# Hash attention into channel mix: wide exps, in-place bits for the first head, joined DMAs and a new order

## The chip, the cores and the metric

One Trainium2 chip, one of its cores. The metric is device time in microseconds of one execution; the same inputs are used each time. The program computes everything in a single launch.

## The reference, cut to what matters

```python
# attention: batch 4, 8 heads, 768 positions, head width 64
q_bits = (einsum('bhsd,dk->bhsk', q, proj) > 0)      # 6 sign bits per row; k_bits alike
mask   = q_bucket[:, :, :, None] == k_bucket[:, :, None, :]
scores = where(mask, scale * q @ k.T, -1e9)
attn   = softmax(scores)                             # over the keys
x      = (attn @ v)  with the heads side by side     # (4, 768, 512)
# channel mix
xk, xr = mixes of x and x shifted by one position, with mu_k and mu_r
k   = max(xk @ w_k, 0)                               # 512 -> 1024
out = sigmoid(xr @ w_r) * ((k * k) @ w_v)
```

A query attends only to the keys whose six sign bits are all equal to its own.

## The kernel before, in words

The 32 heads are handled as 16 pairs, numbered n = 0 to 15, four pairs to a batch. For each pair:

- **Loads.** q and k go to `nat` tiles (three slots), v to `vn`, one DMA each on SP's queue. The first pair is loaded head by head, with k on ACT's queue.
- **Preparation.** The matmul of the scores contracts over 128 partitions: 64 hold q or k times 4 in fp16, six hold the sign bits as large signed numbers, so that one exp with a bias sends every pair of rows with a differing bit to zero. From pair 2 on `add_prep` makes the fp16 value (`hi`, L398) and its rounding error (`lo`, L401) on VectorE, and a transposing DMA on SP turns both (L405). `add_bits` multiplies the turned tile with the projection on TensorE (L427), VectorE takes the signs (L431) and POOL copies them into their six rows, four copies a pair (L443). For pairs in `MERGED` (4 to 15) hi, lo and the DMA treat q and k together, for 2 and 3 one side at a time.
- **The first two pairs** (`FIRSTS`) go through `add_prep_turn` instead: TensorE turns the fp32 tile (L478), ACT copies it negated to SBUF (L483), TensorE multiplies it with the projection (L489), VectorE makes hi (L467) and writes the signs (L497) beside it, TensorE turns the fp16 tile (L512) and VectorE or ACT copies it to its place (L517, L519). Pair 0 goes head by head, pair 1 with both heads at once.
- **Scores and exp.** `add_scores` cuts the 2 x 6 x 768 = 9,216 columns of a pair into nine pieces of 1,024. Each takes two of the eight PSUM banks (`sc` slots 0 to 3), gets three matmuls (L544) and one exp on ACT (L548).
- **PV.** `add_pv` multiplies the exps with v, 12 matmuls to a step and three steps to a head (L571); VectorE divides (L582 to L589). The result is turned by TensorE (pairs 0 to 3 and 15, L599) or a DMA (L605).
- **Mix.** `add_mix` forms xk and xr on VectorE. After four pairs `add_moe` does a batch's channel mix: L659 with relu on ACT (L663) and the square on VectorE (L666), L679 with tanh (L682), L692, and the product (L699) and store (L702). The very last row block is cut into 256, 128 and 128 columns.

At the start TensorE runs matmuls on zeros: `warm0` to `warm13` (L246, one each) and eight `warmb` (L251, two each), which the order places between other work.

Every `add(...)` registers one operation with its engine, an estimate of its duration and what it reads and writes. The list `ORDER` holds the numbers of these operations in the order in which they are issued, and `BANKS` the PSUM place of each operation that takes one. Each engine thus runs its own operations strictly in the order of that list, and waits in that order. So do SP's DMAs. An operation that waits for data or for its PSUM banks holds all that follow on its engine.

In the order before, 22 warm-up matmuls stand ahead of the first L478. On ACT all of `ey0...`, `evt0k0` and `ey1k0` and `evt0k1` stand before the first exp (`sc0_1`); on PE the first L659 stands behind five of the nine score pieces of pair 5 and behind the bits block of pair 6.

## Time and profile before

| | us |
|---|---|
| median of 3 runs (241.7 to 242.24) | 242.17 |
| the profiled execution | 242.0 |
| its span, first to last instruction | 240.2 |
| PE busy | 234.1 |
| ACT busy | 181.9 |
| DVE busy | 179.8 |
| POOL busy | 99.7 |

PE is TensorE's matmuls, PEld its weight loads, DVE VectorE, ACT ScalarE, POOL GpSimd, SP the engine that issues most DMAs. The page cuts the span in 40 slices of 6 us and gives each engine's busy share in tenths. A row of a timeline has start, length, engine, line, operation and, after x, how many like instructions were merged; in brackets stand the idle time before it and who ended it. A row of a group has, behind its count, the busy time, the mean nanoseconds of one, and the engine's idle time before the group with who ended it. A group's mean contains the pipeline's latency, so the pace of a series is read from starts, or from busy time over count.

### The profile page before, as it was taken

The page shows a single profiled execution, that of the slowest core. Times are in us where ns is not written, and L with a number is a line of the kernel's source. Part 1 is how long each engine was busy: PE and PEld are TensorE (multiplying, and loading weights), DVE is VectorE, ACT ScalarE, POOL GpSimd, SP SyncE. Part 2 cuts the span into 40 slices and gives each one's busy share as a digit, 9 for nine tenths or more (in the row PEclk, how much of TensorE's full clock was granted, in tenths as well). Part 3 has the DMA queues.
Part 4 walks back from the last instruction along what each step waited for, and adds up shares of the span by engine and source line. Part 5 has one row for each costly group of instructions (what it writes and reads, how often), then busy time and mean ns, then how long its engine had stood idle before and what let it go on. Part 6 is the DMA issues. An engine that isn't in the chain of part 4 may idle for free.

```text
span 240.2 us, 6251 instructions
## 1 busy us (share of the span) xinstructions
PE 234.1 (97%) x2515; PEld 147.8 (62%) x2532; DVE 179.8 (75%) x388; ACT 181.9 (76%) x242; POOL 99.7 (41%) x148
## 2 busy tenths in 40 slices
PE   8999999999999999999999999999999999999994
PEld 6985776776766565656456656665566564455442
DVE  3488789999998898989868896887167867348232
ACT  2699999999999999889779999677884640256320
POOL 4064979989934899438087302550000000000000
PEclk9999999999999999999999999999999999999999
DMA  6989999999999999988999989401500401210333
GB/s 225 304 222 274 232 242 260 279 197 362 279 253 284 273 213 294 249 302 206 276 163 241 249 177 234 136 0 26 173 0 3 120 3 44 87 46 1 131 135 131
DMA packets 72605, 44.00 MB, mean 183 GB/s; under 512 B 54912, under 2 KB 67584, under 8 KB 72576
## 3 DMA queue, kind: packets, MB, share of 16 engines
q1 hardware_dynamic: 72208, 43.20, 70.9%
q8 instruction: 20, 0.33, 0.6%
q10 hardware_dynamic: 368, 0.39, 0.5%
q14 instruction: 9, 0.07, 0.1%
HBM read 24.12 MB, written 6.29 MB: 127 GB/s over the span
## 4 chain that ended last, share of the span: by engine, by line
PE 92%; ACT 5%; issue 1%; DVE 0%
PE ps_all L544 25%; PE ps_all L692 17%; PE ps_all L659 16%; PE ps_all L571 14%; PE ps_all L679 8%; ACT pt L548 4%; PE ps_all L427 4%; PE ps_all L489 2%; PE ps_all L512 1%; PE ps_all L478 1%; ACT kr L663 1%; PE ps_all L251 1%; PE ps_all L246 1%; PE ps_all L599 1%; PE ps_all L566 1%
## 5 line engine op out<-in xcount | busy, mean ns | idle before, releaser
L548 ACT ACTIVATE pt<-ps_all 128x1024 bf16<-128x1024 f32 x144 | 138.4, 1041 | 10.9 <-PE ps_all L544 10.3
L544 PE MATMUL ps_all<-a 128*128 128x256 f16 (+1 forms) x384 | 79.2, 325 | 0.5 <-ACT pt L548 0.3
L443 POOL COPY a<-bx 6x384 f32<-6x384 f32 x56 | 38.9, 695 | 34.4 <-DVE bx L431 19.6
L544 PEld LDWEIGHTS <-a 128*128 128x128 f16 x384 | 34.0, 98 | 23.5 <-issue 4.6
L659 PE MATMUL ps_all<-xk,wk 128*128 128x384 bf16 x256 | 48.3, 326 | 0.1
L571 PEld LDWEIGHTS <-pt 128*128 128x128 bf16 x1152 | 42.5, 97 | 8.0 <-issue 0.5
L692 PE MATMUL ps_all<-wv,k 128*128 128x512 bf16 (+2 forms) x199 | 45.6, 362 | 0.5
L571 PE MATMUL ps_all<-va,pt 128*128 128x65 bf16 x1152 | 44.8, 193 | 0.0
L663 ACT ACTIVATE kr<-ps_all 128x384 bf16<-128x384 f32 x64 | 29.4, 491 | 16.0 <-PE ps_all L659 14.4
L659 PEld LDWEIGHTS <-wk 128*128 128x128 bf16 x256 | 24.2, 98 | 17.0 <-issue 0.6
L692 PEld LDWEIGHTS <-k 128*128 128x128 bf16 x208 | 19.3, 98 | 18.9 <-issue 0.3
L699 DVE SCALAR_TENSOR_TENSOR os<-rs,ps_all 128x512 f32<-128x512 f32 (+2 forms) x26 | 16.5, 643 | 19.0 <-PE ps_all L692 13.7
L682 ACT ACTIVATE rs<-ps_all 128x512 f32<-128x512 f32 x24 | 14.3, 602 | 20.5 <-PE ps_all L679 14.1
L666 DVE TENSOR_TENSOR k<-kr 128x384 bf16<-128x384 bf16 x64 | 23.2, 389 | 8.3 <-ACT kr L663 8.3
L401 DVE SCALAR_TENSOR_TENSOR nh<-nat,nh 128x1536 f16<-128x1536 f32 (+1 forms) x16 | 27.0, 1694 | 0.2
L679 PE MATMUL ps_all<-wr,xr 128*128 128x512 bf16 x88 | 23.2, 379 | 0.4
L356 POOL TENSOR_TENSOR vt<-vn 128x384 f32<-128x384 f32 x12 | 17.8, 1485 | 12.5 <-DMA vn<-in_v_dram 11.7
L589 DVE TENSOR_TENSOR ob<-ps_all,rc 128x384 bf16<-128x384 f32 x32 | 17.5, 553 | 1.4 <-DMA xt<-ob 0.8
L431 DVE TENSOR_SCALAR bx<-ps_all 128x768 uint16<-128x768 uint16 x14 | 13.4, 956 | 5.3 <-PE ps_all L427 4.7
L398 DVE TENSOR_SCALAR nh<-nat 128x1536 f16<-128x1536 f32 (+1 forms) x16 | 15.8, 985 | 0.3 <-PE ps_all L512 0.2
L679 PEld LDWEIGHTS <-xr 128*128 128x128 bf16 x96 | 9.0, 98 | 9.0
L380 DVE SCALAR_TENSOR_TENSOR va<-ps_all,vn 128x384 bf16<-128x384 f32 x24 | 12.7, 548 | 0.5 <-PE ps_all L375 0.2
(77 smaller groups left out, 188.9 us busy)
## 6 DMA issues: line engine op xcount, KB each, us to landing
vn<-in_v_dram SPq DMA_DIRECT2D x16, 384.0 KB, 5.1
out_dram<-os SPq DMA_DIRECT2D x23, 256.0 KB, 2.3
nat<-in_k_dram SPq DMA_DIRECT2D x15, 384.0 KB, 4.7
nat<-in_q_dram SPq DMA_DIRECT2D x15, 384.0 KB, 5.2
wst<-in_moe_w_k_dram SPq DMA_DIRECT2D x2, 512.0 KB, 7.0
wst<-in_moe_w_r_dram SPq DMA_DIRECT2D x2, 512.0 KB, 5.8
wst<-in_moe_w_v_dram SPq DMA_DIRECT2D x2, 512.0 KB, 4.4
k<-in_moe_w_k_dram SPq DMA_DIRECT2D x1, 512.0 KB, 4.4
```

Source lines behind the costliest of these rows:

```text
L356: e.tensor_tensor(out=vt[:, :, :, 0:E], in0=src[:, :, 0:3, 0:E], in1=src[:, :, 3:6, 0:E], op=ALU.add)
L401: nc.vector.scalar_tensor_tensor(out=nh[:, :, D:P], in0=nat.rearrange("p j (c d) -> p (j c) d", d=D), scalar=QS, in1=nh[:, :, 0:D], op0=AL ...
L443: nc.gpsimd.tensor_copy(side_a[side][n % NAQ][D : D + NB, j, :].bitcast(FP32), bx_t[sx][32 * i : 32 * i + NB, :].bitcast(FP32))
L544: nc.tensor.matmul(ps[:, lo - s * STEP : hi - s * STEP], side_a["k"][sa][:, j, jc * P : (jc + 1) * P], side_a["q"][sa][:, j, q0 : q0 + hi ...
L548: nc.scalar.activation(out=pt_t[sp][:, s * STEP : (s + 1) * STEP], in_=ps_t[plan.slot[nm]], func=AF.Exp, bias=EBIAS, scale=ESC)
L571: nc.tensor.matmul(oo[:, ic * 65 : ic * 65 + 65], pt_t[sp][:, o : o + P], va_t[sa][:, j, jc, 0 : D + 1], start=(not uc and ic == 0 and jc ...
L589: nc.vector.tensor_tensor(out=ob_t[so][:, :, j * D : (j + 1) * D], in0=oo[:, :, 0:D], in1=rc_t[sr][:, 1, :].unsqueeze(2).to_broadcast([P, ...
L659: nc.tensor.matmul(ps[:, 0:HALF], wk_sb[:, d, fc * P : (fc + 1) * P], xk_t[mx[d]][:, h * HALF : (h + 1) * HALF], start=(d == 0), stop=(d = ...
L663: nc.scalar.activation(out=kr_t[sk], in_=sm(nm)[:, 0:HALF], func=AF.Relu, scale=0.5 ** 0.5)
L666: nc.vector.tensor_tensor(out=k2_t[s2][:, h * HALF : (h + 1) * HALF], in0=kr_t[sk], in1=kr_t[sk], op=ALU.mult)
L679: nc.tensor.matmul(sm(nr), xr_t[mx[d]][:, c * P : (c + 1) * P], wr_sb[:, d, :], start=(d == 0), stop=(d == NDC - 1))
L692: nc.tensor.matmul(sm(nv)[:, x0:x1], k2_t[(b * NFC + fc) % NK2][:, c * P : (c + 1) * P], wv_sb[:, fc, x0:x1], start=(fc == 0), stop=(fc == ...
```

## The change

- **Wide exps.** For pairs 1 to 3 (`WIDE`) the 9,216 columns go in six pieces of 1,536 over three PSUM banks; where each starts is given by bank. Dependences on the exps are kept by bank (512 columns) instead of by piece of 1,024.
- **First head in place.** For head 0 of pair 0 (`DIRECT`) the new `add_direct` turns each half (384 columns) of one head to 64 partitions, ACT copies it negated, VectorE writes the fp16 value from PSUM straight into the score operand, a matmul with the projection placed in columns 64 to 69 (`pwx`) puts the bits on partitions 64 to 69, and VectorE writes their signs straight into the operand's rows. There is no fp16 turn for it.
- **Second pair split.** Pair 1 (`TURNED`) is now prepared by `add_prep`: hi and lo per side, then TensorE turns the fp16 tiles and VectorE copies them; its bits come from `add_bits` and POOL's four row copies. It no longer has its own fp32 turn and copy on ACT.
- **Joined DMAs.** `MERGED` begins at pair 2.
- **Warm-up.** `warm` matmuls go from 14 to 8; the separate exp that touched ACT's table and its memset are gone. One of two large memsets of `nh` is gone, two small ones come with `add_direct`.
- **New order** and new bank list. On PE 14 warm-up matmuls stand ahead of the first turn. On DVE the order at the start is: hi of head 1 (k, q), q's two halves with pair 1's q hi after them, k's first half, pair 1's q lo, signs of q half 0, k half 0, q half 1, then k half 1, extraction, sign, pair 1's k hi, extraction, k lo, five copies, hi and lo of pair 2, and then the signs of pair 1. On SP the load of pair 1's q is third, after the two heads of pair 0's q. On PE the first L659 stands behind five score pieces of pair 5, the last of which takes the banks of the eleventh exp after pair 3, and the bits block of pair 6 follows it. The last row block of the output is still cut, but a whole block of 512 columns (`v3_4`) is now the last to be computed and stored.

The wide pieces of pairs 1 to 3, in the order of their exps, with the banks that they take:

```
pair 1: 5-7, 0-2, 5-7, 0-2, 3-5, 5-7
pair 2: 1-3, 5-7, 1-3, 0-2, 4-6, 0-2
pair 3: 4-6, 0-2, 4-6, 0-2, 0-2, 3-5
```

```diff
-    NWARM = 14
+    NWARM = 8
...
-    MERGED = tuple(range(4, 16))
-    FIRSTS = (0, 1)
+    MERGED = tuple(range(2, 16))
+    FIRSTS = (0,)
+    TURNED = (1,)
...
+    DIRECT = ((0, 0),)
+    WIDE = (1, 2, 3)
...
+    pwx = buf([P, 96], FP32, "pwx")
...
+            if n in TURNED:
+                for j in range(2):
...
+                    add("PE", 0.48, tp, r=["idh", ("nhh", side, sh, j), ("nhl", side, sh, j)], w=[(nm,)], take=("sm", nm, 0), name=nm)
+                    add("DVE", DVE_C(S, 2), ev, r=[(nm,)], w=[("a", side, sa, j)] + [("ab", side, sa, j, h) for h in range(2)], give=[nm], name="ev" + nm)
+                continue
...
+    def add_direct(n, side, j):
...
+            def tp(ny=ny, h=h):
+                for c in range(3):
+                    nc.tensor.transpose(sm(ny)[0:D, c * P : (c + 1) * P], nat[:, j, (3 * h + c) * D : (3 * h + c + 1) * D], idf)
+
+            def e32(ny=ny, cols=cols):
+                nc.scalar.activation(out=a32[:, cols], in_=sm(ny)[0:D, 0:HALF], func=AF.Copy, scale=-1.0)
+
+            def hi(ny=ny, cols=cols):
+                nc.vector.tensor_scalar(out=a[0:D, j, cols], in0=sm(ny)[0:D, 0:HALF], scalar1=QS, scalar2=None, op0=ALU.mult)
+
+            def bb(nx=nx, cols=cols):
+                nc.tensor.matmul(sm(nx)[0:96, 0:HALF], pwx[0:D], a32[:, cols], start=True, stop=True)
+
+            def sg(nx=nx, cols=cols):
+                nc.vector.tensor_scalar(out=a[D : D + NB, j, cols].bitcast(U16),
+                                        in0=sm(nx)[D : D + NB, 0:HALF].bitcast(U16).rearrange("p (c e) -> p c e", e=2)[:, :, 1],
+                                        scalar1=0x8000, scalar2=bq, op0=ALU.bitwise_and, op1=ALU.bitwise_or)
...
+    def parts(n):
+        step = 3 * BANK if n in WIDE else STEP
+        return [(lo, lo + step) for lo in range(0, 2 * NSC * S, step)]
...
+            def place(nm=nm, a0=a0, a1=a1):
+                b0 = plan.slot[nm] * (STEP if a1 - a0 == STEP else BANK)
+                return ps_all[:, b0 : b0 + a1 - a0]
...
+        add("POOL", 0.2, lambda: nc.gpsimd.tensor_copy(pwx[0:D, D : D + NB], pw[0:D, 0:NB]), r=["pw0"], w=["pwx"], port=1, name="pjcp")
```

68 lines of the change are left out of this document (45 added, 23 removed), and 119 rows, old and new, of tables (BANKS, ORDER).

## The prediction

> **What bounds the kernel now.** I read the page first: the busy rows, then the 40 slices.
>
> ```profile
> PE 234.1 (97%) x2515; PEld 147.8 (62%) x2532; DVE 179.8 (75%) x388; ACT 181.9 (76%) x242; POOL 99.7 (41%) x148
> ...
> PE   8999999999999999999999999999999999999994
> ...
> DVE  3488789999998898989868896887167867348232
> ACT  2699999999999999889779999677884640256320
> ```
>
> TensorE is never idle for long, and ScalarE and VectorE are full as well in the first third. A busy PE is not proof of a bound, since the ends of matmuls are modelled, so the windows of the first half come next (columns: stretch, its length, then busy time and instructions of PE, PEld, DVE, ACT, POOL, then granted clock, DMA share, GB/s).
>
> ```profile
> 12.00:16.00 4.00, 4.00 (x36) 3.25 (x35) 3.65 (x7) 4.00 (x5) 1.78 (x2) 1.00 0.70 229
> 36.00:42.00 6.00, 6.00 (x97) 3.99 (x95) 5.90 (x11) 6.00 (x8) 5.64 (x6) 1.00 1.09 261
> 48.00:60.00 12.00, 11.99 (x181) 8.13 (x174) 11.56 (x27) 11.79 (x14) 10.93 (x13) 1.00 1.17 279
> 204.00:216.00 12.00, 11.95 (x66) 6.37 (x65) 4.49 (x11) 4.90 (x10) 0.00 (x0) 1.00 0.18 67
> ```
>
> From 36 to 60 us PE, ACT, DVE and POOL are all between 91% and 100%. After 200 us PE alone is full. So the end is PE's work plus whatever PE loses early, and early on PE lives on what ACT gives it: until the first matmul of the channel mix there is nothing to do but scores, PV and bits. The timeline of ACT and PE shows the early rhythm.
>
> ```profile
> 11.60 4.69 ACT L548 ACTIVATE pt<-ps_all 128x1024 bf16<-128x1024 f32 x5
> 16.13 0.85 ACT L483 ACTIVATE pt<-ps_all 128x768 f32<-128x768 f32 x1
> 16.82 2.00 ACT L548 ACTIVATE pt<-ps_all 128x1024 bf16<-128x1024 f32 x2
> 19.06 35.03 ACT L548 ACTIVATE pt<-ps_all 128x1024 bf16<-128x1024 f32 x38 [0.24 <-PE ps_all L544]
> ...
> 57.64 0.65 PE L659 MATMUL ps_all<-xk,wk 128*128 128x384 bf16 x3
> ```
>
> The first exp starts at 11.60. From 19.06 on 38 exps run in 35.03 us without a gap, 0.922 us each. Seven were done before, so the 36 of the first four pairs end at 19.06 + 29 x 0.922 = 45.8 us. The channel mix (L659) starts at 57.64. These three times are the marks that I carry through.
>
> **The change, part by part.**
>
> **Start of PE's real work.**
>
> ```profile
> DMA to landing us min/median/max: 3.0/3.4/3.8
> ...
> 0.73 0.88 SPq L321 DMA_DIRECT2D nat<-in_q_dram  x2
> ...
> 1.19 0.61 PE L251 MATMUL ps_all<-k 128*128 128x256 bf16 x2 [1.19 <-DVE k L243]
> 1.59 0.85 PE L246 MATMUL ps_all<-k 128*128 128x256 bf16 x3
> ...
> 4.99 0.38 PE L246 MATMUL ps_all<-k 128*128 128x256 bf16 x2
> 5.21 1.47 PE L478 MATMUL ps_all<-pt,nat 128*128 128x128 f32 x12
> 6.51 1.41 PE L489 MATMUL ps_all<-pw,pt 128*128 128x12 f32 x12
> ...
> 57.21 0.59 PE L544 MATMUL ps_all<-a 128*128 128x512 f16 x3
> ...
> 5.73 1.64 ACT L483 ACTIVATE pt<-ps_all 128x384 f32<-128x384 f32 x4 [2.19 <-PE ps_all L478]
> ...
> 5.44 0.58 POOL L710 TENSOR_SCALAR npj<-pw 64x6 f32<-64x6 f32 x2 [2.16 <-DMA pw<-in_proj_dram]
> ```
>
> Today 22 warm-up matmuls fill 1.19 to 5.21, 0.2 us apart at first (1.59 less 1.19 for two). The new order puts 8 + 3 x 2 = 14 ahead of the first transpose, so it can start near 1.19 + 14 x 0.215 = 4.2 us; q's first half lands before that (the first loads of q land 3.0 to 3.8 us after issue, which begins at 0.73). PE starts **1.0 us earlier**. The second pair's own fp32 transposes and bit matmuls go and one bits block comes, the first head gets twelve smaller transposes and four matmuls of 384 fp32 columns. No row shows that matmul. A 128-column fp32 transpose takes 0.11 (twelve between 5.21 and 6.51), a 12-column fp32 matmul as much; so the ends are 0.11 and 0.65 (six such transposes), and I take 0.33, three of them for three times the columns. It lies beside VectorE's chain either way, as follows.
>
> **The first head on VectorE.** The three transposes of a half (0.33), their latency (0.2) and ACT's copy (0.41, a quarter of 1.64) make the first half ready for DVE at 4.2 + 0.94 = 5.1 to 5.2. DVE's new order is: two halves of q, hi of pair 1's q, one half of k, lo of pair 1's q, three sign operations, and only then may the first scores go. The durations:
>
> ```profile
> L380 DVE SCALAR_TENSOR_TENSOR va<-ps_all,vn 128x384 bf16<-128x384 f32 x24 | 12.7, 548 | 0.5 <-PE ps_all L375 0.2 <-issue 0.2
> L398 DVE TENSOR_SCALAR nh<-nat 128x1536 f16<-128x1536 f32 x12 | 12.9, 1078 | 0.1
> L401 DVE SCALAR_TENSOR_TENSOR nh<-nat,nh 128x1536 f16<-128x1536 f32 x12 | 23.3, 1941 | 0.1
> L401 DVE SCALAR_TENSOR_TENSOR nh<-nat,nh 128x768 f16<-128x768 f32 x4 | 3.7, 954 | 0.1
> L398 DVE TENSOR_SCALAR nh<-nat 128x768 f16<-128x768 f32 x4 | 2.8, 704 | 0.2 <-PE ps_all L512 0.2
> L517 DVE COPY a<-ps_all 128x768 f16<-128x768 f16 x6 | 3.3, 546 | 0.7 <-PE ps_all L512 0.4
> L497 DVE TENSOR_SCALAR nh<-ps_all 128x36 uint16<-128x36 uint16 x4 | 0.8, 191 | 3.2 <-PE ps_all L489 3.2
> L431 DVE TENSOR_SCALAR bx<-ps_all 128x768 uint16<-128x768 uint16 x14 | 13.4, 956 | 5.3 <-PE ps_all L427 4.7 <-ACT kr L663 0.7
> L443 POOL COPY a<-bx 6x384 f32<-6x384 f32 x56 | 38.9, 695 | 34.4 <-DVE bx L431 19.6 <-issue 9.9 <-POOL vt L356 1.5
> ...
> 10.90 0.79 ACT L519 COPY a<-ps_all 128x768 f16<-128x768 f16 x1
> ```
>
> A 384-column pass out of PSUM on fewer partitions is not among them: between 0.27 (half of L517's 768) and 0.55 (L380); I take 0.5, near L380's. Then 6 x 0.5 + 0.6 (hi) + 0.92 (lo) = 4.5, and the scores may go at 9.8 (0.1 for the late load of pair 1). PE needs until about 9 for what stands before them, so DVE decides. Scores of 1,024 columns take 0.43 (57.21 to 57.64) and 0.16 more until the last is out (0.59): first exp at **10.4 instead of 11.6**.
>
> **Second pair.** Its bits now come late. Before them on DVE stand one half of k, two sign operations, two small extractions (2 x 0.2, L497), hi, lo, five evictions, and then hi and lo of pair 2 in joined form: 2 x 0.5 + 0.4 + 0.6 + 0.92 + 5 x 0.55 + 1.08 + 1.94 = 8.7. So L431 for pair 1 runs from 18.5 to 19.45; its matmuls are ready two microseconds sooner, the queue is what holds it. Two row copies on POOL (0.70 each, L443) are needed before any score of pair 1: 20.85. Scores of 1,536 columns 0.64 (one and a half times 0.43) plus 0.2: first wide exp at 21.7. ACT is done with pair 0 at 10.4 + 9 x 0.922 + 0.8 (one eviction, L519) = 19.5. **ACT waits 2.2 us** there, where before it waited 0.24.
>
> **Wide exps.** From 0.41 at 384 columns to 0.922 at 1,024 is 0.80 ns a column, so 1,536 columns cost 1.33 (upper end 1.38, one and a half times 0.922). 18 x 1.33 = 23.9 against 27 x 0.922 = 24.9: **1.0 us gained**. But two wide buffers take six of the eight banks. Where a score tile's banks overlap those of the exp just before it, PE cannot fill ahead and ACT waits for a whole refill. By the new bank list that is so three times: the sixth tile of pair 1 (banks 5 to 7 after 3 to 5), the fourth of pair 2 (0 to 2 after 1 to 3), the fifth of pair 3 (0 to 2 twice). Each costs 0.64 + 0.16 and the signals, some 0.85: **2.6 us lost**. So the first four pairs end at 21.7 + 23.9 + 2.6 = 48.2 instead of 45.8.
>
> The Trainium skill, ScalarE: Activation LUTs, Rules for kernel authors, budgets about 0.3 us for every ACTIVATE beside 0.83 ns an element. By that nine instructions fewer would save 2.7 us, an estimate from that page, and the end would come 1.7 us sooner than below. This trace disagrees: 0.922 for 1,024 columns leaves 0.07 to 0.10 beside the elements when exps follow one another.
>
> **To the channel mix.**
>
> ```profile
> 31.46 0.77 PE ps_all L427 x16
> ```
>
> Its first matmul stands behind a score tile that needs the eleventh exp after pair 3 done: 48.2 + 11 x 0.922 + 0.45 = 58.8, 1.2 later than 57.64. The seventh pair's bits block, 0.77, now comes after it rather than before. PE has the same work left otherwise: **+1.9 us**. DVE agrees: 8 x 0.5 for the first head, two lo of 0.92 and a bits pass of 0.96 for pair 1 come, seven passes of 0.2 to 0.55 go; that adds over 3 us to an engine that is 96 to 98% busy there.
>
> **The end.**
>
> ```profile
> 234.97 1.71 PE L692 MATMUL ps_all<-wv,k 128*128 128x128 bf16 x20
> ...
> 236.71 0.42 DVE L699 SCALAR_TENSOR_TENSOR os<-rs,ps_all 128x256 f32<-128x256 f32 x1 [0.43 <-PE ps_all L692]
> ...
> 233.50 1.49 DVE L699 SCALAR_TENSOR_TENSOR os<-rs,ps_all 128x512 f32<-128x512 f32 x2 [1.90 <-PE ps_all L692]
> ...
> out_dram<-os SPq DMA_DIRECT2D x23, 256.0 KB, 2.3
> ...
> out_dram<-os SPq DMA_DIRECT2D x1, 128.0 KB, 1.7
> ```
>
> Today the last piece is 256 columns wide: 0.42 on DVE and a 128 KB store of 1.7. In the new order the last is a whole row block of 512: 0.69 (other rows of L699; two make 1.49) and 2.3. That is 0.27 + 0.6 = **+0.9 us**. The pieces of 128 and 256 columns go ahead of it and are hidden.
>
> Edits at nothing: the joined transposes of pairs 2 and 3 (their results wait for banks and DVE), the removed table operation (ACT idles at that point; if uncovered 0.2), the new POOL copy of the projection (0.29, half of L710's 0.58, hidden behind PE's transposes; a late one delays the signs one for one), and the order of loads.
>
> **Sum.** The profiled execution took 242.0 us, its span 240.2, the rest is outside; the median of the runs is 0.17 above it. 242.0 + 1.9 + 0.9 = 244.8; against the median 245.0. I say **244.9**.
>
> **Rivals.**
>
> *Forecast: ACT's chain sets the channel mix late,* 243.2 to 247. The lower end has DVE's passes at 0.27 (2 us sooner at pair 1, less 0.4 that ACT then limits); the upper has 1.38 for a wide exp (0.9) and waits for banks of 1.2 (1.0). Chance 0.50.
>
> *The lag is swallowed (faster).* One mechanism at one place, the first L659: if PE rather than ACT paces the way there, the earlier start counts. For it speaks the 97% of PE, and that the same share holds in every slice. Against it speaks the gapless ACT row. Then PE arrives 1.0 sooner, and about 1 us of prep is gone: 57.64 - 2.0 = 55.6, and the end is 242.0 - 2.0 + 0.77 + 0.27 = 241.0 if the larger store hides its 0.6. The price is ACT's whole 3 us; with the store hidden it decides from L659 before 56.1. Chance 0.22, from 239.8 to 241.6. Halfway, within 0.2% (0.5 us, about what a measurement of this kernel can tell from no change): 0.10.
>
> *The head is not shortened* (it does not do what it says). DVE's queue stands behind the load of pair 1's q, issued third.
>
> ```profile
> DMA to landing us min/median/max: 3.8/4.9/8.9
> ```
>
> Issued at 1.7 it lands between 5.5 and 10.6 by these extremes; at 7.5 hi and lo of pair 1 hold q's signs 1.2 longer, and all marks move: 246.1. Chance 0.12.
>
> *A cold start.* The warm-up rows show 0.21 us a matmul early and 0.11 at 4.99; with eight fewer, and pauses behind ACT and DVE, the fast pitch could come late. Twelve transposes and four fp32 matmuls at double time cost up to 2 us: 247. Chance 0.06. The Trainium skill, TensorE: Matmul & The Clock Gate, What's actually happening, says that the clock opens after about 3.4 us of sustained work; by that rule 14 matmuls (3.0 us) just miss it, so it speaks for this rival. By that rule, the trace agrees: the pitch has halved by 4.99, and no run here shows a shorter warm-up.
>
> **How the numbers follow.** Slower 0.50 + 0.12 + 0.06 = 0.68, same 0.10, faster 0.22. The range leaves out about a tenth on either side: 240.6 to 247.3. The forecast's own range is 243.2 to 247.
>
> **What would show it.** The first exp near 10.4; L431 for pair 1 near 18.5 behind a joined lo; an ACT wait near 2 us before the first wide exp; three ACT waits on L544 near 0.85 among the wide exps; wide exps 1.33 apart; the first L659 near 58.8; a last store of 256 KB. Wrong it is if ACT runs through from pair 0 to pair 1, if the wide tiles never wait, or if L659 comes before 57.6 all the same.

## The result and the profile after

The changed kernel takes 249.93 us (median of 3 runs, 248.65 to 249.94) against 242.17 before: **slower**, ratio 1.0309 [1.0256, 1.0362]. The direction is the one forecast, the size is not: 7.8 us instead of 2.7, and 249.93 lies outside the range. The profiled execution took 249.93, its span is 248.1. Medians below hold all executions of a kernel; ratios leave out those over 1.5% above its fastest, among them the profiled one of `e2_bits_first`, one of 407.93 us in `e16_before_joined`, and two of four in `e14_four_mends`, which has no ratio.

In the changed kernel L609 is the exp (L548 before), L605 the scores (L544), L446 the sign pass (L431), L458 POOL's row copies (L443), L442 the bits' matmul (L427), L719 the channel mix's first matmul (L659), L759 the last product (L699). The page of the changed kernel, with the clock's row:

```profile
PE 234.9 (95%) x2475; PEld 145.2 (59%) x2496; DVE 186.0 (75%) x389; ACT 180.3 (73%) x231; POOL 103.2 (42%) x153
...
PE   7894998999999999999999999999999999999993
...
DVE  4798289999999979998985988896436859545242
ACT  3285788989999999988998898776865642436311
...
PEclk9999799999999999999999999999999999999999
```

PE's busy time is nearly the same (234.9 after, 234.1 before), and the span is 7.9 longer: most of this is idle time of PE, and it stands in the first slices. Two of the windows shown for before:

```profile
36.00:42.00 6.00, 5.56 (x84) 3.60 (x81) 5.91 (x11) 5.14 (x4) 5.50 (x9) 1.00 0.83 189
204.00:216.00 12.00, 11.95 (x84) 6.25 (x83) 8.82 (x20) 4.34 (x8) 0.00 (x0) 1.00 0.06 22
```

From 36 to 42 PE had 6.00 busy and ACT 6.00; now 5.56 and 5.14. After 200 nothing differs for PE. ACT's timeline shows where the gaps are:

```profile
12.18 1.94 ACT L609 ACTIVATE pt<-ps_all 128x1024 bf16<-128x1024 f32 x2 [1.80 <-PE ps_all L605]
...
17.41 4.69 ACT L609 ACTIVATE pt<-ps_all 128x1024 bf16<-128x1024 f32 x5 [0.56 <-PE ps_all L605]
25.38 1.45 ACT L609 ACTIVATE pt<-ps_all 128x1536 bf16<-128x1536 f32 x1 [3.28 <-PE ps_all L605]
27.27 1.45 ACT L609 ACTIVATE pt<-ps_all 128x1536 bf16<-128x1536 f32 x1 [0.44 <-PE ps_all L605]
29.27 4.14 ACT L609 ACTIVATE pt<-ps_all 128x1536 bf16<-128x1536 f32 x3 [0.55 <-PE ps_all L605]
34.30 5.57 ACT L609 ACTIVATE pt<-ps_all 128x1536 bf16<-128x1536 f32 x4 [0.90 <-PE ps_all L605]
40.73 9.51 ACT L609 ACTIVATE pt<-ps_all 128x1536 bf16<-128x1536 f32 x7 [0.86 <-PE ps_all L605]
51.14 15.08 ACT L609 ACTIVATE pt<-ps_all 128x1536 bf16<-128x1536 f32 x15 [0.90 <-PE ps_all L605]
```

Where before one row ran from 19.06 to 54 without a gap, ACT now waits six times from pair 1 on. Seven wide exps in 9.51 are 1.36 each. The last row merges wide and narrow exps: two wide ones end pair 3 at 53.93. The channel mix and the end:

```profile
64.89 0.65 PE L719 MATMUL ps_all<-xk,wk 128*128 128x384 bf16 x3
65.47 0.83 PE L442 MATMUL ps_all<-a,p 128*32 128x512 f16 x16
```

```profile
240.88 0.69 DVE L759 SCALAR_TENSOR_TENSOR os<-rs,ps_all 128x512 f32<-128x512 f32 x1 [0.83 <-DMA out_dram<-os]
...
244.42 0.69 DVE L759 SCALAR_TENSOR_TENSOR os<-rs,ps_all 128x512 f32<-128x512 f32 x1 [0.44 <-issue]
```

The last product ends at 245.11, the span 3.0 later; before it ended at 237.13 and the span 3.1 later. So the larger store adds nothing behind it. The marks, against the prediction:

| us from the span's start | before | predicted | after |
|---|---|---|---|
| first exp | 11.60 | 10.4 | 12.18 |
| first exp of pair 1 | 20.89 | 21.7 | 25.38 |
| pair 3's last exp ends | 45.75 | 48.2 | 53.93 |
| first matmul of the channel mix | 57.64 | 58.8 | 64.89 |
| last matmul ends | 236.68 | 238.6 | 244.33 |

From the channel mix to the last matmul it is 179.0 before and 179.4 after. In this kernel nearly the whole loss (7.25 us) is there when the channel mix begins.

### The profile page after: what moved, and what is told of

Read it like the earlier page. It is cut to its first block, busy times and chain, and to the rows that moved or that the text cites. A ratio compares the mean times of both kernels' runs of the same rounds, so it can differ in the third digit from the quotient of the medians.

```text
span 248.1 us, 6172 instructions
## 1 busy us (share of the span) xinstructions
PE 234.9 (95%) x2475; PEld 145.2 (59%) x2496; DVE 186.0 (75%) x389; ACT 180.3 (73%) x231; POOL 103.2 (42%) x153
## 4 chain that ended last, share of the span: by engine, by line
PE 81%; ACT 7%; DMA 4%; DVE 3%; issue 2%; POOL 1%; ACTq 0%; DVEq 0%; POOLq 0%
PE ps_all L605 21%; PE ps_all L719 17%; PE ps_all L752 16%; PE ps_all L631 11%; PE ps_all L739 8%; ACT pt L609 6%; PE ps_all L442 3%; DMA pw<-in_proj_dram 2%; DMA nat<-in_q_dram 2%; POOL a L458 1%; PE ps_all L484 1%; DVE nh L402 1%; DVE bx L446 1%; PE ps_all L659 1%; PE ps_all L542 1%
## 5 line engine op out<-in xcount | busy, mean ns | idle before, releaser
L609 ACT ACTIVATE pt<-ps_all 128x1024 bf16<-128x1024 f32 (+1 forms) x135 | 138.0, 1102 | 21.3 <-PE ps_all L605 20.8
L605 PE MATMUL ps_all<-a 128*128 128x512 f16 (+1 forms) x384 | 80.1, 328 | 5.0 <-POOL a L458 3.2
L458 POOL COPY a<-bx 6x384 f32<-6x384 f32 x60 | 43.2, 720 | 51.4 <-DVE bx L446 27.7
L605 PEld LDWEIGHTS <-a 128*128 128x128 f16 x384 | 34.2, 98 | 27.2 <-issue 5.5
L631 PEld LDWEIGHTS <-pt 128*128 128x128 bf16 x1152 | 44.0, 98 | 9.1 <-issue 1.1
L719 PE MATMUL ps_all<-xk,wk 128*128 128x384 bf16 x256 | 48.5, 326 | 0.0
L631 PE MATMUL ps_all<-va,pt 128*128 128x65 bf16 x1152 | 46.1, 194 | 0.0
L752 PE MATMUL ps_all<-wv,k 128*128 128x512 bf16 (+2 forms) x195 | 45.0, 361 | 0.7
L723 ACT ACTIVATE kr<-ps_all 128x384 bf16<-128x384 f32 x64 | 30.1, 500 | 17.9 <-PE ps_all L719 14.0
L719 PEld LDWEIGHTS <-wk 128*128 128x128 bf16 x256 | 24.4, 98 | 17.6 <-issue 1.0
L759 DVE SCALAR_TENSOR_TENSOR os<-rs,ps_all 128x512 f32<-128x512 f32 (+2 forms) x26 | 16.3, 642 | 19.9 <-PE ps_all L752 5.5
L402 DVE SCALAR_TENSOR_TENSOR nh<-nat,nh 128x1536 f16<-128x1536 f32 (+1 forms) x16 | 28.1, 1755 | 0.2
L446 DVE TENSOR_SCALAR bx<-ps_all 128x768 uint16<-128x768 uint16 x15 | 14.3, 955 | 4.5 <-PE ps_all L442 3.0
L399 DVE TENSOR_SCALAR nh<-nat 128x1536 f16<-128x1536 f32 (+1 forms) x16 | 15.8, 986 | 0.0
L357 POOL TENSOR_TENSOR vt<-vn 128x384 f32<-128x384 f32 x12 | 14.1, 1175 | 0.7
```

What stands on the lines that cost most here:

```text
L402: nc.vector.scalar_tensor_tensor(out=nh[:, :, D:P], in0=nat.rearrange("p j (c d) -> p (j c) d", d=D), scalar=QS, in1=nh[:, :, 0:D], op0=AL ...
L446: nc.vector.tensor_scalar(out=bx_t[sx][0:rows].bitcast(U16), in0=ps_t[plan.slot[nm]][0:rows, 0:S].bitcast(U16).rearrange("p (c e) -> p c e ...
L458: nc.gpsimd.tensor_copy(side_a[side][n % NAQ][D : D + NB, j, :].bitcast(FP32), bx_t[sx][32 * i : 32 * i + NB, :].bitcast(FP32))
L605: nc.tensor.matmul(ps[:, lo - a0 : hi - a0], side_a["k"][sa][:, j, jc * P : (jc + 1) * P], side_a["q"][sa][:, j, q0 : q0 + hi - lo], start ...
L609: nc.scalar.activation(out=pt_t[sp][:, a0:a1], in_=place(), func=AF.Exp, bias=EBIAS, scale=ESC)
L631: nc.tensor.matmul(oo[:, ic * 65 : ic * 65 + 65], pt_t[sp][:, o : o + P], va_t[sa][:, j, jc, 0 : D + 1], start=(not uc and ic == 0 and jc ...
```

## Two places in the head

**The bits of the first head.** Timeline of the changed kernel, PE, POOL and DVE:

```profile
4.15 1.93 PE L475 MATMUL ps_all<-pt,nat 128*64 128x128 f32 x12
...
6.68 0.40 POOL L768 COPY pwx<-pw 64x6 f32<-64x6 f32 x1 [4.18 <-DMA pw<-in_proj_dram]
...
7.13 1.53 PE L484 MATMUL ps_all<-pt,pwx 64*96 64x384 f32 x4 [1.05 <-POOL pwx L768]
...
9.40 1.53 PE L484 MATMUL ps_all<-pt,pwx 64*96 64x384 f32 x4
...
10.32 0.56 DVE L487 TENSOR_SCALAR a<-ps_all 6x384 uint16<-6x384 uint16 x1 [0.90 <-PE ps_all L484]
...
11.54 1.03 PE L605 MATMUL ps_all<-a 128*128 128x512 f16 x5
```

PE's real work begins at 4.15, as forecast, and gains nothing: the matmul with the projection (L484) waits 1.05 for POOL's copy, and that for a load which now stands behind pair 1's q on SP. And it costs more than its upper end: each of the four operations runs as two instructions, so four instructions in 1.53 are two operations at 0.72 or more, where 0.33 was taken and 0.65 was the bound. From 7.13 on PE works without a gap up to the first scores at 11.54, and the sign pass at 10.32 waits for it: PE leads here, not VectorE.

**The rows of the second pair.** DVE, POOL and PE, then the same place in `e3_rows_alone`, where hi and lo of pair 3 (L399, L402) come later:

```profile
18.56 1.76 DVE L402 SCALAR_TENSOR_TENSOR nh<-nat,nh 128x1536 f16<-128x1536 f32 x1
20.24 0.95 DVE L446 TENSOR_SCALAR bx<-ps_all 128x768 uint16<-128x768 uint16 x1
...
21.17 0.95 DVE L399 TENSOR_SCALAR nh<-nat 128x1536 f16<-128x1536 f32 x1
21.32 3.14 POOL L458 COPY a<-bx 6x384 f32<-6x384 f32 x2 [6.80 <-DVE muk L276]
22.16 1.94 DVE L402 SCALAR_TENSOR_TENSOR nh<-nat,nh 128x1536 f16<-128x1536 f32 x1
...
24.52 0.82 PE L605 MATMUL ps_all<-a 128*128 128x512 f16 x4 [3.24 <-POOL a L458]
```

```profile
20.04 0.95 DVE L446 TENSOR_SCALAR bx<-ps_all 128x768 uint16<-128x768 uint16 x1
...
21.12 1.06 POOL L458 COPY a<-bx 6x384 f32<-6x384 f32 x2 [6.80 <-DVE muk L276]
22.23 0.82 PE L605 MATMUL ps_all<-a 128*128 128x512 f16 x4 [1.16 <-POOL a L458]
```

The two copies take 3.14 beside hi and lo (1.17 and 1.92) and 1.06 alone, and end 0.36 behind lo. The forecast had 0.70 each, the mean of 56 copies that mixes both cases. The Trainium skill, SBUF — State Buffer, SBUF: two separate sides, says that a VectorE instruction with two inputs in SBUF and a GpSimd one that reads SBUF lock each other out for whole instructions; lo reads nat and nh, and the second copy, which lies beside it, agrees: 1.92 instead of 0.50. The first copy lies beside hi, which reads nat alone, so that sentence does not give its 1.17.

## The experiments

Theory Q: the queues ahead of pair 1 set the loss and it passes to the end. Theory B: the wide pieces' banks and the order behind them set it. Theory C: the clock. Orders are shown by the operations' names.

**Projection early.** On SP the projection's load goes ahead of pair 1's q.

```diff
-ldq0q0, ldq0q1, ldq1q, ldpw1, ldv0
+ldq0q0, ldq0q1, ldpw1, ldq1q, ldv0
```

> Edit: SP issues its small load of the projection ahead of pair 1's q instead of behind it; all else as in the changed kernel. Theory Q (the queues ahead of pair 1 set the loss, and what is lost at the first wide exp is lost at the end): the projection lands near 5.4 instead of 6.55 us, the copy of it on POOL starts near 5.4 instead of 6.68, the first exp near 11.0 instead of 12.18, the first wide exp near 24.2 instead of 25.38, and the time falls by 1.2 us from 249.9 to 248.7, or to 247.5 if PE's idle stretch gets too short to halve its clock. Theory B (banks and the later order set the loss, early delays are swallowed): first exp earlier as well, but the first matmul of the channel mix and the time move by less than 0.4 us.

249.02 us, 1.0229 [1.0174, 1.0285]. First exp 11.78, first exp of pair 1 25.20, channel mix 64.03. The first exp comes 0.4 sooner, but other profiles with the same head have it between 11.86 and 12.35, so little can be read from that. In this profile the turn (L475) takes 2.66 instead of 1.93, its twelve transposes standing 0.21 apart (three such steps, then 0.11 to 0.19, in the changed kernel): the clock opens later here, and that eats into the gain. The row copies end 0.8 sooner; the scores behind them then fall into a half clock and take 1.46 instead of 0.82, so pair 1's first exp is only 0.2 sooner. The channel mix moves by 0.9, between Theory Q's 1.2 and Theory B's 0.4.

**Bits first.** On DVE the sign pass of pair 1 goes ahead of hi and lo of pair 2.

```diff
-hi2, lo2, bx1
+bx1, hi2, lo2
```

> Edit: on VectorE the sign pass of pair 1 goes ahead of hi and lo of pair 2. Theory Q: the pass starts near 18.9 instead of 20.24 us; the two row copies then lie beside hi and lo of pair 2 and stay slow (1.57 each), so the first wide exp comes 1.5 to 2.3 us earlier (23.1 to 23.9 instead of 25.38); PE's idle stretch falls under 3 us, its clock stays whole, and the time falls by 1.5 to 3.3 us, to 246.6 to 248.4. Theory B: hi and lo of pair 2 are later by one pass, its bits wait for banks anyway, and the time stays within 0.5 us of 249.9 (248.7 if only the clock is saved).

252.2 us, ratio 1.0254 [1.0149, 1.0358]. First exp of pair 1 23.83, 1.5 sooner, but pair 4's first exp waits 4.42, and the channel mix is at 68.54. In this profile the scores there wait 4.47 for POOL's row copies, which stand behind a wait of 4.15 for a load of v, and the clock is at half for 6.8 us around them. The run leaves open what the move is worth.

**Rows alone.** hi and lo of pair 3 go behind the first division.

```diff
-bx1, hi3, lo3, rc0, ob0
+bx1, rc0, ob0, hi3, lo3
```

> Edit: on VectorE hi and lo of pair 3 go behind the first head's division instead of right behind the sign pass of pair 1, so that POOL's first two row copies of pair 1 have no such pass beside them. Theory Q with a shared cause (POOL's copies are slow because of VectorE's hi and lo beside them): the two copies take 0.5 to 0.7 us each instead of 1.57, the first wide exp comes 1.7 to 2.1 earlier (near 23.5), the time falls by 1.7 to 3 us. Rival (the copies have their own pace, two passes over six rows are slow by themselves): they take 1.5 each as before, the first wide exp stays at 25.4, and the later lo of pair 3 makes the time equal or up to 1 us longer.

248.85 us, 1.0251 [1.0191, 1.0311]. First exp of pair 1 23.09 (2.3 sooner), channel mix 62.26 (2.6 sooner), last matmul 243.03: only 1.3 sooner. Half of the gain is lost behind the channel mix; a transposing DMA is waited for there (1.1 us) that after's waits do not have. And 1.3 is what the next experiment puts down to the clock: this profile has a mean clock of 1.000, that of the changed kernel 0.991. The changed kernel's one execution at 1.000 took 248.65, the four here, at 0.998 to 1.000, took 248.63 to 250.58, so that nothing of the 2.3 us is seen at the end. This speaks against Q.

**Keep warm.** Five pairs of filler matmuls go into PE's wait ahead of pair 1.

```diff
+warmb1, warmb0, warmb4, warmb5, warmb6, sc1_5
```

> Edit: five pairs of matmuls on zeros, which stood later in PE's order, are put into its wait ahead of the first wide score tile; no work is added. Theory C (the wait of over 3 us halves PE's clock, and the waits of 0.44 and 0.55 us before the second and third wide exp come from that): granted clock 1.0 from 24 to 30 us instead of 0.72, those two waits under 0.1, and the time 0.9 to 1.3 us shorter, 248.6 to 249.0. Rival: the two waits are refills of three banks and stay, and the time stays at 249.9 within 0.4.

Windows of the changed kernel, then of this one:

```profile
20.00:24.00 4.00, 1.04 (x16) 0.69 (x14) 3.96 (x5) 2.10 (x3) 2.62 (x2) 1.00 0.77 165
24.00:30.00 6.00, 5.48 (x63) 3.76 (x64) 0.85 (x3) 3.63 (x3) 3.94 (x8) 0.72 1.12 233
```

```profile
20.00:24.00 4.00, 2.21 (x25) 1.59 (x24) 3.83 (x5) 1.86 (x3) 2.86 (x2) 1.00 0.81 167
24.00:30.00 6.00, 5.47 (x73) 3.65 (x77) 2.38 (x5) 4.85 (x4) 5.42 (x9) 1.00 1.06 237
```

Granted clock is the third column from the end. 0.72 over 6 us is half speed for 3.4 of them (the dip), behind PE's wait of 3.24. With fillers the dip and ACT's waits of 0.44 and 0.55 are gone, and the last matmul ends 1.7 sooner in this profile (248.24). The median is 249.74, 1.0262 [1.0202, 1.0322], for in its other executions the mean clock was 0.990 to 0.993: the dip still comes in some. The changed kernel itself took 249.93 and 249.94 at 0.991 and 248.65 at 1.000. Theory C holds for about 1.3 us, an estimate from these few executions.

**Two mends, and more of them.** Projection early and rows alone together:

```diff
-ldq1q, ldpw1; bx1, hi3, lo3, rc0, ob0
+ldpw1, ldq1q; bx1, rc0, ob0, hi3, lo3
```

> The changed kernel with two moves together: the projection's load ahead of the load of pair 1's q, and hi and lo of pair 3 on DVE put off behind the first division. Theory Q (the queues ahead of pair 1 set the loss, and it passes to the channel mix) expects the two gains to add in the marks: first exp near 11.8, the two row copies near 1.1 instead of 3.1, first wide exp 22.2 to 22.6 instead of 25.38, pair 3's end near 50.5 instead of 53.93, first matmul of the channel mix near 61.4 instead of 64.89, and the time 246.0 to 247.8. Rival, later work swallows it (putting off hi and lo of pair 3 only moves the debt behind the channel mix): first wide exp as above, but time 248.5 or more, as with the second move alone.

248.89 us, 1.0245 [1.02, 1.0289]; first exp of pair 1 23.06, channel mix 62.23, both as with rows alone, last matmul 243.40. The time is the rival's, but whether the two add is not tested: the first exp is at 11.96 as with rows alone (11.97), since the turn takes 2.77 in this profile, with the half pace of its transposes lasting to its end.

Head 0 turned whole as before, with the projection early:

```diff
-    DIRECT = ((0, 0),)
+    DIRECT = ()
```

> The changed kernel with head 0 of pair 0 prepared by the turn again (whole 768 columns: fp32 turn, ACT's copy, bits at 12 columns, hi, signs and extraction, fp16 turn, copies) instead of in place, the projection's load ahead of pair 1's q as in the first experiment, which it is to be held against. Theory H (the in-place head with its four bits matmuls of 0.72 and six passes of half a head is itself longer than the turn) expects the first exp at 10.6 to 11.2 instead of 11.78, the signs of pair 1 on DVE 1 us sooner, and first wide exp 24.0 to 24.6 instead of 25.2; time 248.2. Rival: the loads and DVE's other work set the start, and the in-place head is no longer: first exp 11.6 to 12.2, time 249.0 as in the first experiment.

First exp 10.97 instead of 11.78, first exp of pair 1 23.37, channel mix 62.88, so the in-place head is itself 0.8 longer than the turn, as Theory H says. Still the profiled execution takes 248.73 (0.990 mean clock) and another 249.86 (0.984), two more 253.11 and 253.47 (both 0.965): a median of 251.49 and a ratio of 1.0387 [1.0302, 1.0471], which holds the two long ones; the first two alone are 1.027 of before. Against 1.0229 with only the projection early, no gain is seen at the end.

Four mends, the edits of the first, third and fourth experiment and of the last one together:

> The changed kernel with four mends of its head together: projection's load early, head 0 by the turn, hi and lo of pair 3 put off behind the first division, five filler pairs in TensorE's wait ahead of pair 1. Wide pieces, split second pair and joined transposes stay. If the gains add: first exp near 11.0, first exp of pair 1 21.5 to 22.2, pair 3's end 49.5 to 50.2 (27.9 later, no half clock), first matmul of the channel mix 60.5 to 61.2, time 245.5 to 246.5. Rival, a floor behind the first matmul (seen where hi and lo of pair 3 were put off: only half of the gain reached the end): time 247.5 to 248.5.

Windows of the head:

```profile
8.00:12.00 4.00, 4.00 (x26) 3.17 (x24) 1.83 (x6) 1.76 (x4) 3.85 (x12) 0.51 1.05 374
12.00:18.00 6.00, 6.00 (x40) 5.02 (x39) 2.73 (x5) 3.67 (x4) 1.53 (x2) 0.50 0.77 219
```

252.22 us, and the profile (251.16) tells little of the mends: the clock is at half from 8 to 18. The fastest execution took 247.99. No execution with a mend of the head comes under 247.6.

**Narrow pieces.** Pairs 1 to 3 in pieces of 1,024 at the wide pieces' places.

```diff
-    WIDE = (1, 2, 3)
+    WIDE = ()
```

> The changed kernel with pairs 1 to 3 in nine pieces of 1,024 columns over two banks again, in the order of the pieces that free the same exps, all else as it is. Theory B (the three-bank pieces cost refills where their banks overlap) expects the three ACT waits of 0.86 to 0.90 at 34.3, 40.7 and 51.1 to vanish (2.66 less), 27 x 0.921 instead of 18 x 1.359 for the exps (0.41 more), so first exp of pair 1 to pair 3's end 26.3 instead of 28.55 where PE is warm, first matmul of the channel mix near 62.6 and the time near 247.7. Rival: the waits come from the order of PE's queue (PV and bits blocks ahead of the scores) and stay with any width: 28.5 to 29 and a time of 249.9 or more.

256.69 us, 1.0546 [1.0477, 1.0616]. From pair 1's first exp to pair 3's end 32.7 instead of 28.55; PE waits 1.16 and 1.48 with the bits' matmul for a bank that an exp holds. With the turned head, early projection and put-off rows as well:

> The changed kernel with all four undone at once: projection's load early, hi and lo of pair 3 put off, two-bank pieces, head 0 by the turn. What stays of the change: fewer warm-ups, the second pair split, joined DMAs and the new order otherwise. Theory Q with B and H: gains add, 0.9 + 2.3 + 2.2 + 0.8 = 6.2 at the first matmul of the channel mix, so near 58.7, and a time of 243.5 to 245, within 1% of the kernel before. Rival, later work swallows it: first matmul near 59 but a time of 246 or more, since the new order behind it costs by itself.

255.48 us, 1.0519 [1.0474, 1.0565]; its profile shows a first exp at 13.62, with the clock at half until 20.4. Both miss by 9 to 12 us. They do not show that wide is better: before runs narrow pieces without a gap, in an order made for them. They show that this order does not bear this other width.

**Other banks.** The same order with other banks for 23 tiles (the expectation says 22; the filler tiles and small ones among them), so that no wide tile overlaps the one before it.

```diff
-pair 1: 3-5, 5-7; pair 2: 1-3, 5-7, 1-3, 0-2; pair 3: 0-2, 0-2
+pair 1: 3-5, 0-2; pair 2: 3-5, 0-2, 3-5, 0-2; pair 3: 0-2, 4-6
```

These are the wide tiles that overlap, with their neighbours; the sixth of pair 3 moves too, from 3-5 to 0-2.

> The changed kernel with other PSUM banks for 22 tiles and the same order: of the three overlaps of a wide tile with the one before it none is left (sixth of pair 1 in 0-2 after 3-5, second to fourth of pair 2 in 0-2, 3-5, 0-2, fifth of pair 3 in 4-6 after 0-2). Theory B (the waits of 0.86 to 0.90 are refills of overlapping banks) expects all three to vanish, or the last to shrink to what the sign pass of pair 4 holds, so first exp of pair 1 to pair 3's end 25.8 to 26.5 instead of 28.55, first matmul of the channel mix 62.2 to 63.0 instead of 64.89, time 247.4 to 248. Rival: PE reaches these scores late by its own order, and ACT waits 0.6 to 0.9 there with any banks: 249.9.

254.58 us, 1.047 [1.0412, 1.0528]. The three waits stay at their tiles and grow to 1.39, 1.23 and 2.77, so overlapping banks alone are not the cause. Why, PE's rows show; first the changed kernel, then this one:

```profile
30.85 0.81 PE L605 MATMUL ps_all<-a 128*128 128x512 f16 x4 [0.30 <-DVE ob L649]
31.59 0.83 PE L442 MATMUL ps_all<-a,p 128*32 128x512 f16 x16
32.35 0.51 PE L659 MATMUL ps_all<-idb,ob 128*128 128x128 bf16 x6
...
32.87 0.53 PE L631 MATMUL ps_all<-va,pt 128*128 128x65 bf16 x12
...
33.46 0.81 PE L605 MATMUL ps_all<-a 128*128 128x512 f16 x4
```

```profile
32.42 0.34 PE L626 MATMUL ps_all<-vsu,tiny 128*128 128x390 bf16 x1 [0.70 <-DVE bx L446]
...
33.81 5.48 ACT L609 ACTIVATE pt<-ps_all 128x1536 bf16<-128x1536 f32 x4 [1.39 <-PE ps_all L605]
```

In the changed kernel PE is busy without a gap from 30.85: scores, bits, turn of a result, PV, and only at 33.46 the scores that ACT waits for, the very time at which ACT's last exp ends (29.27 + 4.14 = 33.41) and frees the bank. In this row order and bank hold them equally. With other banks the bits' own bank becomes the wait. So **the scores of these tiles also go ahead** of bits and turn (and the turn ot0 takes another bank):

```diff
-sc1_0, bits2, ot0, oo1_1, sc1_1
+sc1_0, sc1_1, bits2, ot0, oo1_1
-sc2_3, bits3, ot1, sc2_0
+sc2_3, sc2_0, bits3, ot1
```

> The changed kernel with the other banks of the earlier run and with two scores moved in TensorE's order: the sixth wide tile of pair 1 directly behind the fifth, ahead of the bits of pair 2 and the turn of pair 0's result; the fourth of pair 2 directly behind the third, ahead of the bits of pair 3. Third overlap as in that run. If banks and order each hold these scores (either alone leaves the wait): the waits near 34.3 and 40.7 go, pair 3's end 1.5 to 1.8 earlier than with the banks alone (54 instead of 55.6). If banks alone were the cause, they would have gone already; if something else (the operands, POOL's rows) holds them, waits of 0.8 to 1.4 stay at the same two tiles.

ACT's timeline:

```profile
25.56 8.16 ACT L609 ACTIVATE pt<-ps_all 128x1536 bf16<-128x1536 f32 x6 [3.28 <-PE ps_all L605]
35.82 5.63 ACT L609 ACTIVATE pt<-ps_all 128x1536 bf16<-128x1536 f32 x4 [2.10 <-PE ps_all L605]
```

Six wide exps now follow each other without a gap, so banks and order did hold that tile together, and the fourth of pair 2 does not wait either. But the wait comes back at the next tile, 2.10 us, and at the fifth of pair 2, 1.68, and pair 3 ends at 56.85, not the 54 expected; 254.99 us, 1.0491 [1.0445, 1.0536]. Two wide tiles and two PV accumulators are all eight banks; the bits (two banks) and the turn (one) of each pair have to stand in the place of one of these, wherever they are put.

**Halves.** Before's head (pairs 0 and 1 prepared and ordered as before, 22 warm-ups) with the rest of the change:

```diff
-    NWARM = 8
+    NWARM = 14
...
-    FIRSTS = (0,)
-    TURNED = (1,)
+    FIRSTS = (0, 1)
+    TURNED = ()
...
-    DIRECT = ((0, 0),)
+    DIRECT = ()
```

> Head of before, rest of the change: pairs 0 and 1 prepared as before (turned whole, 22 warm-ups, before's order of loads and engines up to the last exp of pair 0), then wide pieces, joined DMAs and the changed order. Theory Q (the head costs 4.5 and the rest passes it on) expects the first exp of pair 1 near 21 instead of 25.38, pair 3's end 48.5 to 49.5, first matmul of the channel mix 59.5 to 60.5, time 244.5 to 246. Rival, the rest is bound elsewhere (DVE's joined hi and lo, POOL's rows): pair 1 starts near 21 but pair 3's end comes after 51, and the time is 247 or more.

252.29 us, 1.0368 [1.0317, 1.0418], spoilt: DVE's pass over mu_k stood ahead of the first division and waited for a load that before's head issues late, and PE waited 2.49 for the division. Mended, with that pass ahead of the first mix instead:

> The head of before with the rest of the change once more, with VectorE's pass over mu_k put behind the first divisions (it held the whole queue for mu_k's load until 28.3 in the run before) and two filler pairs out of the head. Theory Q expects first exp 11.6 to 12.2, first exp of pair 1 21.3 to 22, pair 3's end 28 later (27.5 to 28.6 as in the changed kernel), so 49.0 to 50.5, first matmul of the channel mix 60 to 61.5, time 245 to 247. Rival, the rest is bound elsewhere: pair 3's end after 51.5 and 248 or more.

250.2 us, 1.0292 [1.0244, 1.034]. First exp 11.88, first exp of pair 1 21.96, yet pair 3's end at 51.47 and the channel mix at 62.70: ACT waits 0.52, 1.01, 0.60, 0.68, 0.90 and 0.73 among the wide exps. Theory Q misses by 3 to 5 us in the time; the rival (bound elsewhere) holds, but for pair 3's end just ahead of its 51.5. The profiled execution, at a mean clock of 1.000, took 248.49, where the changed kernel took 248.65 at 1.000. The other way round, the change's head with before's order and pieces from pair 1 on (`WIDE = ()`, before's banks):

> Head of the change, rest of before: pair 0 with head 0 in place, pair 1 split with its rows copied by POOL, the changed loads and order up to the last exp of pair 0; then two-bank pieces in before's order and banks (the joined transposes of pairs 2 and 3 stay, five filler pairs stand in PE's wait ahead of pair 1). Theory Q expects first exp of pair 1 near 25, from there to pair 3's end before's 24.9 without waits: 50.0 to 50.5, first matmul of the channel mix 62 to 62.5 and a time of 246.5 to 247.2, so the head's share of the loss is 4.5 and the rest's 2.5 to 3. Rival: before's order is tuned to early bits and stalls behind a late pair 1: pair 3's end after 52, time 248.5 or more.

248.34 us, 1.0226 [1.0176, 1.0276]. First exp of pair 1 22.80, with waits of 2.02, 1.32 and 0.78 behind it; pair 3's end 52.09. That is the rival's mark (after 52) with a time just under its 248.5; Theory Q's start near 25 did not come about. The profiled execution has the dip too (from 26.3 to 29.7), and all four have a mean clock of 0.991 to 0.993.

**Joining alone.** Before with `MERGED` from pair 2 on, hi, lo and the DMA at the place of the second of the two sides:

```diff
-    MERGED = tuple(range(4, 16))
+    MERGED = tuple(range(2, 16))
```

> The kernel before with q and k of pairs 2 and 3 joined (one hi, one lo and one transposing DMA a pair, each at the place of the second of the two before), nothing else. If the joining is free, as the prediction costs it: ACT runs through from 19.06, all marks and the time as before, 241.7 to 242.7. Rival: the bits of pair 2 come later, since q's side has to wait for k's, and ACT waits 0.5 to 2 us at pair 2; time 242.7 to 244.5.

Timeline, L543 being the scores and L547 the exp there:

```profile
29.33 0.38 PE L543 MATMUL ps_all<-a 128*128 128x512 f16 x1 [0.28 <-POOL a L442]
29.80 18.57 ACT L547 ACTIVATE pt<-ps_all 128x1024 bf16<-128x1024 f32 x20 [0.34 <-PE ps_all L543]
```

244.84 us, 1.0089 [1.0065, 1.0113]. ACT's gapless row has gaps of 0.34 and 0.33, the channel mix comes at 59.06, 1.4 later. What the prediction put at nothing costs about 2 us by itself; the rival expected waits at pair 2, and they are there, only smaller than its 0.5. And before's head with the rest of the change **without the joining** (`MERGED` from 4 on, the sides in before's order):

> The run with the head of before and the rest of the change once more, with q and k of pairs 2 and 3 prepared one side at a time as in the kernel before, at its places in VectorE's and SP's order. What stays of the change: wide pieces in pairs 1 to 3, their banks and the order from pair 1 on. If the joining costs here what it costs alone: pair 3's end 0.7 to 1.4 earlier (50.1 to 50.8), time 248 to 249. If the order with the wide pieces is what holds the rest: pair 3's end 51 to 51.6 and a time of 249.5 to 250.5, as with the joining.

ACT's timeline:

```profile
21.87 1.45 ACT L609 ACTIVATE pt<-ps_all 128x1536 bf16<-128x1536 f32 x1 [0.68 <-PE ps_all L605]
23.84 5.48 ACT L609 ACTIVATE pt<-ps_all 128x1536 bf16<-128x1536 f32 x4 [0.52 <-PE ps_all L605]
30.21 5.48 ACT L609 ACTIVATE pt<-ps_all 128x1536 bf16<-128x1536 f32 x4 [0.90 <-PE ps_all L605]
36.84 9.51 ACT L609 ACTIVATE pt<-ps_all 128x1536 bf16<-128x1536 f32 x7 [1.15 <-PE ps_all L605]
47.25 16.00 ACT L609 ACTIVATE pt<-ps_all 128x1536 bf16<-128x1536 f32 x16 [0.90 <-PE ps_all L605]
```

248.02 us, 1.0238 [1.0199, 1.0277]. Both pair 3's end, 50.04, and the time are about what was expected if the joining costs here what it costs alone: 0.5%, though the two intervals overlap. Wide pieces and new order by themselves cost 2.4%, 5.8 us. The last matmul ends at 240.76, 4.1 late; the other 1.7 stand at the end, where the last products wait 2.63 for earlier stores to free their buffers. The changed kernel shows only 0.3 of such a lag behind its last matmul.

**Fewer warm-ups in the kernel before**, 16 instead of 22 ahead of the first turn:

```diff
-    NWARM = 14
+    NWARM = 8
```

> The kernel before with 16 instead of 22 warm-up matmuls ahead of the first turn, nothing else. The prediction's first step says that PE's real work then starts up to 1.0 earlier: first turn at 4.1 to 4.4 instead of 5.21. If the first turn sets the start and nothing swallows it: first exp 10.8 to 11.2 instead of 11.60 and a time of 241.4 to 241.8. Rival: the loads (q's second half is read by VectorE at 4.98) and the projection hold the next steps: first exp 11.4 or later, time 242.2. Third: the clock opens late with a shorter warm-up: 243 or more.

Timeline, the turn and the bits of the first heads:

```profile
4.57 2.12 PE L477 MATMUL ps_all<-pt,nat 128*128 128x128 f32 x12
6.53 1.41 PE L488 MATMUL ps_all<-pw,pt 128*128 128x12 f32 x12
```

242.02 us against 242.64, 0.9967 [0.9939, 0.9995]. The turn starts 0.64 sooner and takes 2.12 instead of 1.47; the next step is at 6.53 instead of 6.51 and the first exp at 11.61 instead of 11.60. The marks show no gain, as the rival says, but for the third's reason: the first seven of the twelve transposes stand 0.21 apart and the others 0.11, where before all stand 0.11 apart, so the clock opens later in this profile. One profile can't tell whether the shorter warm-up did that. The interval lies below 1 by 0.0005, and the marks give no cause for a gain, so no kernel tried is clearly ahead of the one before.

## Why the prediction was right in sign and wrong in size

The loss by halves, as ratios:

| | before from pair 1 on | change from pair 1 on |
|---|---|---|
| before's head | 1 | 1.0292 (without joining 1.0238) |
| the change's head | 1.0226 (joining included; that alone 1.0089) | 1.0309 |

The forecast added a late pair 1 to three bank waits. The table shows two halves, either of which costs 2 to 3% (intervals from 1.0176 to 1.034), and together hardly more than the larger. With the change's order behind it the head counts for almost nothing: before's head brings pair 1 forward by 3.4 us and the time stays (250.2 against 249.93). So Theory Q, that the head sets the loss, falls; the larger part is what comes with the wide pieces and their order, and the prediction priced that at 2.6 less 1.0.

By its steps, with what each adds to the 5.0 us that are missing:

- **Start of PE's real work**: as forecast, 4.15. As a gain it is wrong; in the profile with fewer warm-ups the turn runs longer, at half pace for its first part, and nothing comes sooner.
- **The first head on VectorE**: this step failed. 12.18 instead of 10.4, +1.8. "PE needs until about 9 for what stands before them, so DVE decides" is wrong: PE comes to the first scores at 11.54. Its eight bits instructions take 3.06 where four times 0.33 were counted, and 1.05 goes on the wait for the projection. "A late one delays the signs one for one" was written, and the load's place on SP was not counted. What the late load costs by itself stays open, since the profiles with the load early have a turn at half pace that hides it.
- **Second pair**: the joined lo and the queue behind it were right (the words of the sum name three passes of half a head, its 2 x 0.5 counts two, and two there are); the sign pass at 20.24 instead of 18.5 is the first head's lag. Pair 0's end slips 0.8 more (ACT waits 0.56 within it), and the row copies at 1.57 on average instead of 0.70 give +1.1 more of wait (3.28, not 2.2).
- **Wide exps**: 1.36 instead of 1.33, +0.5; the three waits fell on the three tiles named, 0.90, 0.86 and 0.90 for 0.85, though the reason given (banks) is only half of it, so that the match in size is partly luck. Not foreseen were the clock's dip, 0.44 + 0.55, and 0.4 besides. Together +2.0 to pair 3's end.
- **Edits at nothing**: the joined transposes cost 0.9% where they stand alone, and about 0.5% with before's head. In the marks of the changed kernel that price is not separate; it is covered by the other waits.
- **To the channel mix and the end**: +0.4 up to it, 0.4 less of PE's work behind it, and 0.65 less at the end, since the store hides in the 3 us that follow the last product anyway. Sum: 1.8 + 0.8 + 1.1 + 2.0 + 0.4 - 0.4 - 0.65 = 5.05.

Of the rivals, "the head is not shortened" came true with its sign and at another place: not pair 1's q but the load behind it. "Cold start" shows in the changed kernel for three transposes (0.21 apart, then 0.11), which the wait for the projection covers, and for longer in some profiles of other kernels. The lag was not swallowed.

What stays open: how the 5.8 us with before's head divide between wide pieces and order. By the marks, 4.1 of them go with ACT's waits (0.68 + 0.52 + 0.90 + 1.15 + 0.90 = 4.15, against 0.24 before) and 1.7 with the wait at the end; what the order adds to each wait is not shown but for the tiles of the two bank experiments. Wide pieces in an order made for them were not tried, nor was a single wide pair.

## What to carry to other kernels

Here an order and a bank list belong together: half of the other schedule put into it cost nearly as much as the whole, so a price per edit, added up, was no forecast where several engines are full. Two tiles of three banks plus two accumulators leave no bank for anything else: look not only for overlaps of the large tiles but for where the small ones live. Before a mean of many instructions is used as a price, look what stands beside them at the place in question. And before two profiles are compared mark by mark, look whether the clock halved in one of them alone.

## What the runs showed of the hardware

- A wait of 3.24 us on PE was followed by half a clock for 3.4 us. Waits of 3.24 to 3.26 at the same place have such a stretch at their end or behind it in the profiles with the projection early, the turned head and the other banks, but not in those with narrow pieces or the moved scores; with before's order behind the change's head a wait of 1.95 has it. Which executions of one kernel meet the dip varies, and it is worth about 1.3 us here. Longer stretches at half clock last 6.8 us (bits first) and 10.2 us (four mends), two and three times the 3.4. The Trainium skill, TensorE: Matmul & The Clock Gate, What's actually happening, tells of free-running windows of about 3.4 us: the stretch agrees. By its rule a busy window opens the clock; the run with four mends shows PE busy for 10 us of 10 (its ends are modelled) at 0.50 to 0.51, which that rule alone does not give. About two thirds of the instructions there are transposes.
- A matmul of 384 fp32 columns runs as two instructions and takes 0.72 or more, the bound from six transposes being 0.65.
- POOL's copy of 6 x 384 takes 0.50 alone, 1.17 beside VectorE's hi and 1.92 beside lo.
